# Conformer block on one core: transposed keys kept by pairs of tiles, and the scores of the last 32 keys computed in one run with the products of those keys

## Chip, core and metric

The kernel runs on one core of a Trainium2 chip. The metric is the device time of one launch in microseconds. Before the change three runs gave 1850.52, 1851.56 and 1852.84 us (median 1851.56). One further execution was taken with the hardware profiler; it took 1851.06 us, with a span of 1846.9 us between its first and its last profiled instruction.

## What is computed

Two sequences (B = 2) of T = 4000 tokens of width D = 512 go through one Conformer block, all in bf16:

```python
h = _silu(_layernorm(x) @ w_ff1_a) @ w_ff1_b;  x1 = x + 0.5 * h
h = _layernorm(x1);  q, k, v = h @ w_q, h @ w_k, h @ w_v
p = _softmax(einsum('btd,bsd->bts', q, k) * D ** -0.5)
x2 = x1 + einsum('bts,bsd->btd', p, v) @ w_o
# then a gated convolution of width 3 with normalization over all tokens (x3),
# a second feed-forward half step (x4), and a last _layernorm
```

The part that matters here is the attention: every token's query against all 4000 keys of its sequence. 4000 is 31 tiles of 128 keys and one tile of 32, so there are 32 key tiles and the last one has only 32 keys.

## The kernel before

**Stages.** The work goes in 16 chunks of 512 tokens (the eighth and the sixteenth have 416), eight per sequence. All chunks go through the first feed-forward half (until about 430 us of the span). Then comes attention, chunk by chunk, g = 0 to 15, mixed with the projections and convolutions of earlier chunks (about 440 to 1346 us), then the rest of the convolution and the second feed-forward half.

**Attention.** `attention` (line 2255) runs for each chunk g over 32 steps kt, one per key tile. Chunk 0 is done plainly, tile by tile (`scores`, line 1822). In the other chunks four key tiles make a "quad", and the scores of a quad are formed with seven products in place of eight (`score_quad`, line 2184, four steps; `half_quad`, line 2146, does it for tiles 0 and 1). The seven products use the transposed keys `hT` themselves and sums of them, `KF`, which VectorE forms once per sequence (`k_sums`, line 2101), which are stored in DRAM (`kfd`) and loaded again for each chunk (`k_stream`). Within `score_quad`, product 5 (`KF` by a sum of queries, both in the region `xt`) goes into bank 1 of PSUM (called `s` in the profile), ScalarE copies it away, and products 6 and 7 wait for additions of VectorE. Exponentials go into the region `sums`, and the products with the values (`pv`, line 1962) go into banks `y`, and one into the fourth bank of `s`.

**The tile of 32 keys.** Its scores are computed by `tail_scores` (line 2438): 16 matmuls in which the stationary operand is only 32 columns wide, four of them side by side in the array, each for a quarter of the queries (`tile_position=(0, j * REST)`; the profile calls this form 128*32). They go into bank 1; ScalarE takes the exponential into `pq` (region `wff`), which is stored in DRAM (`pqd`) and read back by four DMAs into `ptail`, laid out for the next use. That use is `pv_rest` (line 1982) with tail = 1: products with the values of those 32 keys, contracted over 32 rows, three of them side by side for u = 0 and three for u = 1 (`tile_position=(j * REST, 0)`; form 32*128). `pv_rest` for chunk g runs in `late_second` (line 2333), that is at step kt = 1 of chunk g + 1, and once more at kt = 6 for one product that uses all rows. `tail_scores` for chunk g runs at kt = 24 of chunk g (21 in chunk 0, 16 in the last).

**Transposed keys.** The normalized rows of all tokens are stored in DRAM (`keysd`). `key_queries` (line 2469) brings one tile of 128 keys into `hT` with one DMA transpose on SP's queue, [128 keys, 512] into [128, 4, 128]. `hT` of a chunk is laid out tile by tile. The first 20 tiles of sequence 0 come during the first feed-forward half, the rest in its last chunk and at the start of attention; the tiles of sequence 1 replace those of sequence 0 during g = 7 and 8 (`keys_swap`, line 2402).

**Order.** Nothing is issued in the order of the code. `Plan` (line 112) collects all operations with their dependences and estimated costs and lists them anew for each engine; operations on TensorE that belong to one accumulation (`inc` false up to the last) make one block and are not separated. Each engine then runs its list in order, so an instruction that waits holds back all behind it on its engine; this holds for the DMAs that SP issues, too. Nearly every instruction is recorded under line 95, so groups are told apart by the names of regions and by form.

The functions that the diff touches and their callers:

Of the kernel before, what the change touches and what calls it, by code (L numbers as in the profile page):

```python
# [15 lines left out]
TILE = 128  # L16
TPC = 4
# [3 lines left out]
FC = F // 128  # L21
# [538 lines left out]
class Conformer:  # L560
# [35 lines left out]
    def memory(self):  # L596
# [55 lines left out]
        self.b_hT = [[A.buf("hT%d" % t, t * 4096 + j * 1024, 1024) for j in range(TPC)]  # L652
                     for t in range(TCB)]
# [62 lines left out]
        self.hv = A.view(TCB * 4096, 2 * PAIRS * D).rearrange("p (n k e d) -> p n k e d", k=2, e=2, d=HD)  # L716
        self.hq = A.view(2048, QUADS * 2048).rearrange("p (q u r e j k) -> p q u r e j k", q=QUADS, u=2, r=2, e=2, j=2)
        self.hh = A.view(0, 1024).rearrange("p (r e n) -> p r e n", r=2, e=2)
        self.kfd = nc.dram_tensor("kfd", [B, QUADS + 1, 128, 1536], BF16, kind="Internal").ap()
# [1038 lines left out]
    def row_max(self, qc):  # L1758

        S, s = self.S, qc % 2  # L1760
        for ti in range(TPC):
            for kc in range(TCB):
                ps, b_ps = self.sbank()
                out = ps[0:TILE, :].rearrange("p (t k) -> p t k", t=TPC)
                for cc in range(DC):
                    self.mm(out, self.qT[s][:, cc, ti * TILE:(ti + 1) * TILE], self.hT[kc][:, :, cc, :],
                            cc == 0, cc == DC - 1, [self.b_qT[s][cc]] + self.b_hT[kc], b_ps)
# [54 lines left out]
    def scores(self, g, kt, bank=None):  # L1822
        s, W = g % TCB % 2, width(g)
        kc, kj = divmod(kt, TPC)
        ps, b_ps = bank or self.sbank()
        for cc in range(DC):
            self.mm(ps[:, 0:W], self.hT[kc][:, kj, cc, :], self.qT[s][:, cc, 0:W],
                    cc == 0, cc == DC - 1 and not self.any_score,
                    [self.b_hT[kc][kj], self.b_qT[s][cc]], b_ps)
# [270 lines left out]
    def k_sums(self, g, q, step):  # L2100
# [5 lines left out]
        if q < 0:  # L2106
            a11, a12, a21, a22 = [self.hh[:, r, e] for r in range(2) for e in range(2)]
            s1, s2, s4 = [self.KF[n][:, m, 0].rearrange("p j k -> p (j k)") for m in range(3)]
# [36 lines left out]
    def half_quad(self, g, step):  # L2145
# [5 lines left out]
        m5, b_m5 = self.m5h[:, 0:hw], self.b_m5h  # L2151
        part = lambda r, e: (lambda j: self.hT[0][:, r, 2 * e + j, :], self.b_hT[0][r])
        form = lambda m: (lambda j: self.KF[0][:, m, 0, j], self.b_KF[0][m])
# [88 lines left out]
    def attention(self, old, hook, between):  # L2242

        S = self.S
        for g in range(NCK):
            W, plain = width(g), g == 0
            for kt in range(KT):
# [157 lines left out]
    def keys_swap(self, g, kt):  # L2405
# [31 lines left out]

    def tail_scores(self, g):

# [3 lines left out]
        ps, b_ps = self.bank(1)  # L2443
        hT, b_hT = self.hT[TCB - 1][:, TPC - 1], self.b_hT[TCB - 1][TPC - 1]
        parts = [(slice(j * REST, (j + 1) * REST), slice(j * n, (j + 1) * n)) for j in range(4)]
# [4 lines left out]
        if self.any_score:  # L2450
            for j, (r, q) in enumerate(parts):
# [3 lines left out]
        self.store(self.pqd[:, 0:n], self.pq[:, 0:n], [self.b_pq], [self.b_pqd])  # L2455
        k = S.dsems[self.nxt("ld", 16)]
        src = self.pqd[:, 0:n].rearrange("(j k) q -> k j q", j=4)
        S.dma("SP", k, *[lambda e, r=r: e.dma_start(self.ptail[r, 0:W].rearrange("p (j q) -> p j q", j=4), src)
                         for r, q in parts], reads=[self.b_pqd], writes=[self.b_ptail])

# [8 lines left out]
    def key_queries(self, b, kt):  # L2469
        kc, kj = divmod(kt, TPC)  # L2470
        src, rd = self.key_source(b, kt)
        self.transpose(self.hT[kc][:, kj], src, rd, [self.b_hT[kc][kj]])

# [461 lines left out]
    def program(self, any_score):  # L2935
# [37 lines left out]
        def key_rest():  # L2973

            for k in range(self.PRELOAD, 28):
                yield 8, lambda k=k: self.key_queries(0, k)
            for k in range(15):
                yield 11, lambda k=k: self.key_values(0, k)
            for k in range(28, KT):
                yield FC, lambda k=k: self.key_queries(0, k)  # L2980
# [5 lines left out]
        def ff1(c):  # L2986
            def hook(f):
# [369 lines left out]
```

## Time and profile before

| | |
|---|---|
| three timed runs | 1850.52, 1851.56, 1852.84 us |
| profiled execution | 1851.06 us (span 1846.9 us) |
| TensorE (PE) busy | 1827.6 us, 16082 matmuls |
| VectorE (DVE) busy | 1491.3 us |
| ScalarE (ACT) busy | 1364.9 us |
| DMA | 231.09 MB, mean 125 GB/s |
| DMA transposes of 128 keys | 62 out of `keysd`, 2 out of `tailsd` |

Times are microseconds from the start of the span. In a timeline row stand the start, the duration, the engine, the line, the operation, out<-in by region names, the form and the count; in brackets follows idle time before the instruction with what ended it. A matmul is written as (rows*columns of the array), then the moving operand. Consecutive matmuls overlap, so the time that one costs is read from the distance between starts, not from its duration. For a group, the first number after the bar is its busy time, the second the mean duration in ns of one instruction.

### The profile page before, as it was taken

How to read it: one execution, taken by the hardware profiler on the slowest of the kernel's cores; microseconds unless marked ns; L12 is line 12 of the kernel's file. 1: busy time of each engine (PE TensorE's matmuls, PEld its weight loads, DVE VectorE, ACT ScalarE, POOL GpSimd, SP SyncE). 2: the span in 40 equal slices, each digit the busy share in tenths (PEclk: the TensorE clock that was granted, in tenths of full speed). 3: DMA queues.
4: the chain of work that ended last, by engine and by line, in shares of the span. 5: the costliest groups of instructions: out<-in, count | busy, mean ns of one | idle time of the engine just before them, and what ended most of it. 6: DMA issues, size and time to landing. Idle time of an engine off the chain costs nothing.

```text
span 1846.9 us, 40836 instructions
## 1 busy us (share of the span) xinstructions
PE 1827.6 (99%) x16082; PEld 1518.8 (82%) x16168; DVE 1491.3 (81%) x3240; ACT 1364.9 (74%) x2433; POOL 144.3 (8%) x357
## 2 busy tenths in 40 slices
PE   9999999999999999999999999999999999999998
PEld 6888888866888888889878888888876888888887
DVE  8889898868766877677876777777779989889886
ACT  6887777755656877787777877887768788777775
POOL 2000000000000000000100000000011000000010
PEclk9999999999999999999999999999999999999999
DMA  7332344287645655458954444543476222211211
GB/s 200 87 91 85 83 111 100 70 245 226 173 144 143 189 153 157 125 151 178 241 146 136 123 116 117 146 122 111 124 218 171 56 69 77 73 47 48 64 44 45
DMA packets 317722, 231.09 MB, mean 125 GB/s; under 512 B 191362, under 2 KB 288325, under 8 KB 317268
## 3 DMA queue, kind: packets, MB, share of 16 engines
q1 hardware_dynamic: 316996, 228.15, 45.7%
q8 instruction: 129, 2.11, 0.5%
q14 instruction: 69, 0.57, 0.1%
q10 hardware_dynamic: 528, 0.26, 0.0%
HBM read 131.15 MB, written 56.22 MB: 101 GB/s over the span
## 4 chain that ended last, share of the span: by engine, by line
PE 95%; DVE 2%; ACT 1%; DMA 1%; issue 1%; SPq 0%; DVEq 0%; ACTq 0%
PE y L95 50%; PE s L95 45%; DVE work L95 1%; ACT work L95 0%; DVE wff L95 0%; ACT sums L95 0%; DMA work<-work 0%; DMA pqd<-wff 0%; ACT keys L95 0%; DVE xt L95 0%; DVE sums L95 0%; DVE s L95 0%; DMA xt<-kfd 0%; DVE keys L95 0%; ACT xt L95 0%
## 5 line engine op out<-in xcount | busy, mean ns | idle before, releaser
L95 ACT ACTIVATE sums<-s 128x512 bf16<-128x512 f32 (+4 forms) x498 | 291.3, 586 | 145.9 <-PE s L95 143.0
L95 ACT ACTIVATE keys<-s 128x512 bf16<-128x512 f32 (+3 forms) x275 | 156.9, 574 | 132.7 <-PE s L95 101.6
L95 DVE TENSOR_TENSOR sums<-sums 128x512 bf16<-128x512 bf16 (+3 forms) x528 | 201.3, 399 | 54.6 <-ACT sums L95 42.2
L95 PE MATMUL y<-work,keys 128*128 128x256 bf16 x1920 | 244.4, 273 | 0.0
L95 PE MATMUL s<-sums 128*128 128x256 bf16 (+1 forms) x1428 | 212.6, 272 | 0.1
L95 PE MATMUL y<-sums,keys 128*128 128x256 bf16 (+1 forms) x1440 | 210.6, 270 | 0.0
L95 PE MATMUL y<-wff,keys 128*128 128x256 bf16 (+2 forms) x1590 | 209.4, 276 | 0.1
L95 ACT ACTIVATE work<-xt,work 128x512 bf16<-128x512 bf16 x260 | 199.5, 784 | 9.5 <-DVE work L95 7.8
L95 PEld LDWEIGHTS y<-work,keys 128*128 128x128 bf16 x1920 | 187.8, 98 | 22.4
L95 PE MATMUL y<-work,wff 128*128 128x256 bf16 (+3 forms) x1324 | 197.2, 272 | 0.1
L95 DVE TENSOR_TENSOR keys<-keys 128x1024 bf16<-128x1024 bf16 (+2 forms) x264 | 170.7, 660 | 22.9 <-ACT keys L95 20.2
L95 PE MATMUL s<-work,keys 128*128 128x256 bf16 (+4 forms) x1329 | 184.6, 275 | 1.0
L95 PEld LDWEIGHTS y<-wff,keys 128*128 128x128 bf16 (+1 forms) x1592 | 151.4, 98 | 30.2 <-issue 3.4
L95 DVE BATCH_NORM_STATS2 work<-xt 128x6 f32<-128x512 bf16 x251 | 164.3, 681 | 2.4 <-DMA xt<-in_x_dram 1.7
L95 PEld LDWEIGHTS s<-sums 128*128 128x128 bf16 x1428 | 139.0, 98 | 22.5 <-DVE s L95 0.4
L95 PEld LDWEIGHTS y<-sums,keys 128*128 128x128 bf16 x1440 | 138.1, 98 | 21.3 <-issue 2.9
L95 POOL TENSOR_TENSOR work<-work 128x4 f32<-128x4 f32 (+3 forms) x108 | 91.2, 845 | 764.8 <-DVE work L95 741.8
L95 PE MATMUL s<-xt,keys 128*128 128x256 bf16 (+1 forms) x924 | 142.3, 270 | 1.2 <-DVE s L95 1.1
L95 PEld LDWEIGHTS y<-work,wff 128*128 128x128 bf16 x1324 | 127.3, 98 | 17.6 <-DVE wff L95 0.4
L95 PE MATMUL y<-sums,xt 128*128 128x256 bf16 (+1 forms) x960 | 140.7, 270 | 0.3 <-DVE sums L95 0.3
L95 PEld LDWEIGHTS s<-work,keys 128*128 128x128 bf16 (+1 forms) x1348 | 107.7, 97 | 34.9 <-ACT sums L95 2.2
L95 PE MATMUL s<-xt 128*128 128x256 bf16 (+1 forms) x893 | 131.4, 270 | 1.3 <-DMA xt<-kfd 0.9
(163 smaller groups left out, 3343.9 us busy)
## 6 DMA issues: line engine op xcount, KB each, us to landing
xt<-kfd SPq DMA_DIRECT2D x98, 384.0 KB, 3.2
xt<-v12d SPq DMA_DIRECT2D x105, 256.0 KB, 3.1
xd<-xt SPq DMA_DIRECT2D x28, 512.0 KB, 2.7
xt<-xd SPq DMA_DIRECT2D x28, 512.0 KB, 3.8
out_dram<-xt SPq DMA_DIRECT2D x14, 512.0 KB, 2.9
xt<-in_x_dram SPq DMA_DIRECT2D x13, 512.0 KB, 4.4
dcvd<-wff SPq DMA_DIRECT2D x48, 128.0 KB, 2.9
keys<-dcvd SPq DMA_DIRECT2D x12, 512.0 KB, 3.7
```

The source lines that it names most:

```text
L95: return getattr(eng, self.name)(*self.args, **self.kw)
```

## The change

Two things change, and the rest of the diff adapts addresses to them.

1. `hT` is laid out by pairs of tiles, [2 pairs, 4, 2 tiles, 128], and a new `key_pair` brings 256 keys with one DMA transpose, [256, 512] into [128, 4, 256]. The two last tiles of a sequence are still brought singly. The times at which the plan's input lists these loads shift by a few steps, and the 32-key tile of sequence 1 is listed for step 5 of chunk 7 where it was step 6 of chunk 8. The sums of keys now read runs of 128 elements where they read 256.
2. `tail_scores` of chunk o + 1 is called in `late_second(o)`, right behind `pv_rest` of chunk o, and `pv_rest` no longer ends its accumulations with `inc`, so that both make one block for the plan. The four DMAs that read `pqd` back are listed eight steps later. Chunk 0 keeps its call at kt = 21.

```diff
-        self.hT = [A.view(t * 4096, 2048).rearrange("p (t c k) -> p t c k", t=TPC, c=DC)
-                   for t in range(TCB)]
+        self.hTp = [A.view(t * 4096, 2048).rearrange("p (m c x) -> p m c x", m=2, c=DC) for t in range(TCB)]
+        self.hT = [A.view(t * 4096, 2048).rearrange("p (m c r k) -> p m r c k", m=2, c=DC, r=2) for t in range(TCB)]
...
-    def pv_rest(self, g, tail, ns):
+    def pv_rest(self, g, tail, ns, inc=None):
...
-                        False, u == 1, [b, b_x], b_ps, skip_group_check=True, **at)
+                        False, u == 1, [b, b_x], b_ps, inc=inc, skip_group_check=True, **at)
...
-            a11, a12, a21, a22 = [x[:, :, r, e].rearrange("p u j k -> p u (j k)") for r in range(2) for e in range(2)]
-            s1, s2, s4 = [self.KF[n][:, m].rearrange("p u j k -> p u (j k)") for m in range(3)]
+            a11, a12, a21, a22 = [x[:, :, r, e] for r in range(2) for e in range(2)]
+            s1, s2, s4 = [self.KF[n][:, m] for m in range(3)]
...
-                if kt == (21 if g == 0 else 24 if g < NCK - 1 else 16):
+                if g == 0 and kt == 21:
                     self.tail_scores(g)
...
         self.pv(o, 7, self.group(GROUPS - 1))
-        for tail in range(2):
-            self.pv_rest(o, tail, (7, 3, 2))
+        self.pv_rest(o, 0, (7, 3, 2))
+        if o < NCK - 1:
+            self.pv_rest(o, 1, (7, 3, 2), False)
+            self.tail_scores(o + 1, 8)
+        else:
+            self.pv_rest(o, 1, (7, 3, 2))
...
-            for k in range(KT):
-                if (6 + k * (2 * KT - 20) // KT if k < KT - 1 else KT + 6) == at:
-                    self.key_queries(1, k)
+            for k in range(0, KT - 2, 2):
+                if 7 + k * (2 * KT - 20) // KT == at:
+                    self.key_pair(1, k)
+            for k in range(2):
+                if at == (7 + (KT - 2) * (2 * KT - 20) // KT, 5)[k]:
+                    self.key_queries(1, KT - 2 + k)
...
-    def tail_scores(self, g):
+    def tail_scores(self, g, back=0):
...
+        def load():
+            k = S.dsems[self.nxt("ld", 16)]
+            S.dma("SP", k, *[lambda e, r=r: e.dma_start(self.ptail[r, 0:W].rearrange("p (j q) -> p j q", j=4), src)
+                             for r, q in parts], reads=[self.b_pqd], writes=[self.b_ptail])
+
+        if back:
+            self.after(back, load)
+        else:
+            load()
...
+    def key_pair(self, b, kt):
+        kc, kj = divmod(kt, TPC)
+        src, rd = self.keys_at(b, kt * 128, 256)
+        self.transpose(self.hTp[kc][:, kj // 2], src, rd, self.b_hT[kc][kj:kj + 2])
...
-            for k in range(self.PRELOAD, 28):
-                yield 8, lambda k=k: self.key_queries(0, k)
+            for k in range(self.PRELOAD, 28, 2):
+                yield 8, lambda k=k: self.key_pair(0, k)
...
-                if TCB < c < NCK - 1 and f % 4 == 2:
-                    k = (c - TCB - 1) * 4 + f // 4
+                if TCB < c < NCK - 1 and f % 8 == 2:
+                    k = (c - TCB - 1) * 4 + f // 8 * 2
                     if k < self.PRELOAD:
-                        self.key_queries(0, k)
+                        self.key_pair(0, k)
```

What this does to the lists of the engines is shown at two places. The first is TensorE's list at kt = 1 of chunk 4 (641 to 643 us of the profile before). `y<-xt,keys` and `s<-xt,keys` are the tile before the last (`pv_rest` with tail = 0), `y<-wff,keys` and `s<-wff,keys` the 32-key products, `s<-work,keys 32x128` the scores of the 32 keys; `s<-xt 128x256` with three more is product 5 of the first quad (into bank 1), the pair `s<-xt` and the two `s<-work,keys` are products 6 and 2 of `half_quad`, and `s<-xt,keys` behind the wait for VectorE is its product 7. Before:

```order
L95 MATMUL s<-xt 128x256 [waits cnt_ACT,dma_7]
L95 MATMUL s<-xt 128x256 x3
L95 MATMUL s<-xt,keys 128x256
L95 MATMUL y<-xt,keys 128x256
L95 MATMUL s<-xt 128x256 [waits cnt_ACT]
L95 MATMUL s<-xt 128x256
L95 MATMUL s<-work,keys 128x256 x2
L95 MATMUL y<-wff,keys 128x256 [waits dma_4]
L95 MATMUL s<-wff,keys 128x256
L95 MATMUL y<-wff,keys 128x256 x2
```

After those come the two last 32-key products, `y<-sums,keys 128x256 x6` and product 7. Now the same stretch reads:

```order
L95 MATMUL y<-wff,keys 128x256 [waits dma_9]
L95 MATMUL s<-wff,keys 128x256
L95 MATMUL y<-wff,keys 128x256 x2
L95 MATMUL s<-wff,keys 128x256
L95 MATMUL y<-wff,keys 128x256
L95 MATMUL s<-work,keys 32x128 [waits cnt_ACT]
L95 MATMUL s<-work,keys 32x128 x15
L95 MATMUL y<-sums,keys 128x256 x2
L95 MATMUL s<-xt 128x256 [waits cnt_ACT]
L95 MATMUL s<-xt 128x256
L95 MATMUL s<-work,keys 128x256 x2
L95 MATMUL s<-xt 128x256 [waits cnt_ACT,dma_7]
```

The 16 score matmuls stand directly behind the six 32-key products; products 6 and 2 and product 5 have moved behind both, and four `y<-sums,keys` follow before product 7. At kt = 24 the 16 matmuls are gone; in the feed-forward halves TensorE's list is the same as before.

The second place is SP's list of DMAs around kt = 24 to 31 of chunk 14 (about 1298 to 1309 us). `pqd<-wff` stores the exponentials of the 32 keys, `wff<-pqd` reads them back, `xt<-kfd` loads the sums of a quad of keys, `xt<-v12d` sums of values. Before:

```order
L95 DMA xt<-xd 128x2048 [waits dma_36]
L95 DMA pqd<-wff 128x128 [waits cnt_ACT]
L95 DMA xt<-v12d 128x2x512 [waits cnt_PE,dma_0]
L95 DMA wff<-pqd 32x4x128 [waits dma_37]
L95 DMA wff<-pqd 32x4x128 x3
L95 DMA xt<-kfd 128x1536 [waits cnt_PE,dma_1]
```

And now the same stretch with what follows it, up to the load of the last chunk's 32-key exponentials:

```order
L95 DMA xt<-xd 128x2048 [waits dma_37]
L95 DMA xt<-v12d 128x2x512 [waits cnt_PE,dma_1]
L95 DMA xt<-kfd 128x1536 [waits cnt_PE]
L95 DMA dcvd<-wff 128x512 [waits cnt_DVE]
L95 DMA xt<-v12d 128x512 [waits cnt_PE,dma_4]
L95 DMA xt<-v12d 128x2x512 [waits cnt_PE,dma_6,dma_11]
L95 DMA pqd<-wff 128x104 [waits cnt_ACT]
L95 DMA xt<-kfd 128x1536 [waits cnt_PE]
L95 DMA dcvd<-wff 128x512 [waits cnt_DVE]
L95 DMA lrowd<-wff 1x512 [waits cnt_DVE]
L95 DMA work<-lrowd 128x4 [waits dma_39]
L95 DMA xt<-kfd 128x1536 [waits cnt_PE]
```

The four reads of `pqd`, with their wait for the store, no longer stand ahead of the load of `kfd`; they come behind this piece, with other work between the store and them.

More of the change, by code (lines that the diff above doesn't have):

```diff
@@ L649, in memory @@
         self.b_h = [A.buf("h%d" % k, o + k * 1024, 1024) for k in range(KT)]
-        self.hT = [A.view(t * 4096, 2048).rearrange("p (t c k) -> p t c k", t=TPC, c=DC)
-                   for t in range(TCB)]
-        self.b_hT = [[A.buf("hT%d" % t, t * 4096 + j * 1024, 1024) for j in range(TPC)]
+        self.hTp = [A.view(t * 4096, 2048).rearrange("p (m c x) -> p m c x", m=2, c=DC) for t in range(TCB)]
+        self.hT = [A.view(t * 4096, 2048).rearrange("p (m c r k) -> p m r c k", m=2, c=DC, r=2) for t in range(TCB)]
+        self.b_hT = [[A.bufs("hT%d" % t, [(t * 4096 + j // 2 * 2048 + cc * 512 + j % 2 * 256, 256) for cc in range(DC)])
+                      for j in range(TPC)]
                      for t in range(TCB)]
@@ L1763, in row_max @@
                 ps, b_ps = self.sbank()
-                out = ps[0:TILE, :].rearrange("p (t k) -> p t k", t=TPC)
+                out = ps[0:TILE, :].rearrange("p (m r k) -> p m r k", m=2, r=2)
                 for cc in range(DC):
-                    self.mm(out, self.qT[s][:, cc, ti * TILE:(ti + 1) * TILE], self.hT[kc][:, :, cc, :],
+                    self.mm(out, self.qT[s][:, cc, ti * TILE:(ti + 1) * TILE], self.hT[kc][:, :, :, cc, :],
                             cc == 0, cc == DC - 1, [self.b_qT[s][cc]] + self.b_hT[kc], b_ps)
@@ L2107, in k_sums @@
             a11, a12, a21, a22 = [self.hh[:, r, e] for r in range(2) for e in range(2)]
-            s1, s2, s4 = [self.KF[n][:, m, 0].rearrange("p j k -> p (j k)") for m in range(3)]
+            s1, s2, s4 = [self.KF[n][:, m, 0] for m in range(3)]
             b_x = self.b_hT[0][0:2]
@@ L2455, in tail_scores @@
         self.store(self.pqd[:, 0:n], self.pq[:, 0:n], [self.b_pq], [self.b_pqd])
-        k = S.dsems[self.nxt("ld", 16)]
         src = self.pqd[:, 0:n].rearrange("(j k) q -> k j q", j=4)
-        S.dma("SP", k, *[lambda e, r=r: e.dma_start(self.ptail[r, 0:W].rearrange("p (j q) -> p j q", j=4), src)
-                         for r, q in parts], reads=[self.b_pqd], writes=[self.b_ptail])
+        def load():
[6 more added lines that the diff above has]
+            load()
     def key_source(self, b, kt):
@@ L2973, in key_rest @@
         def key_rest():
-            for k in range(self.PRELOAD, 28):
-                yield 8, lambda k=k: self.key_queries(0, k)
+            for k in range(self.PRELOAD, 28, 2):
+                yield 8, lambda k=k: self.key_pair(0, k)
             for k in range(15):
                 yield 11, lambda k=k: self.key_values(0, k)
-            for k in range(28, KT):
+            yield FC, lambda: self.key_pair(0, 28)
+            for k in range(30, KT):
                 yield FC, lambda k=k: self.key_queries(0, k)
```

12 lines of the change are left out of this document (6 added, 6 removed).

## The prediction

> **What bounds the kernel now.** I read the page first: the busy times, the slices and the chain that ended last.
>
> ```profile
> span 1846.9 us, 40836 instructions
> PE 1827.6 (99%) x16082; PEld 1518.8 (82%) x16168; DVE 1491.3 (81%) x3240; ACT 1364.9 (74%) x2433; POOL 144.3 (8%) x357
> PEclk9999999999999999999999999999999999999999
> PE 95%; DVE 2%; ACT 1%; DMA 1%; issue 1%; SPq 0%; DVEq 0%; ACTq 0%
> ```
>
> TensorE is the bound from end to end, at full granted clock. Idle it can lose at most 1846.9 - 1827.6 = 19.3 us in the whole span. The change lists TensorE's work differently in attention alone, so I read that stretch by windows, and two stretches of the first feed-forward half, where key transposes run beside it.
>
> ```profile
> 440.00:1346.00 906.00, 900.39 (x8198) 756.04 (x8242) 683.23 (x1559) 668.72 (x1247) 55.98 (x212) 1.00 0.56 149
> 200.00:300.00 100.00, 100.00 (x919) 89.64 (x917) 90.32 (x185) 78.62 (x132) 8.05 (x8) 1.00 0.43 102
> 300.00:400.00 100.00, 99.95 (x870) 84.95 (x869) 82.44 (x172) 66.78 (x114) 7.91 (x14) 1.00 0.46 126
> ```
>
> After the length stand the busy times of PE, PEld, DVE, ACT and POOL. TensorE idles 906.0 - 900.4 = 5.6 us in attention and nothing in the feed-forward stretch. A gain must therefore come out of matmul time that looks busy, or out of those 5.6 us.
>
> **The price of a narrow run.** Busy hides something here: the ends of matmuls are modelled, so I take distances between starts. Two timelines of PE, first a plain run of 12, then one chunk's 16 score matmuls of the 32 keys:
>
> ```profile
> 836.01 1.47 PE L95 MATMUL y<-sums,work 128*128 128x256 bf16 x12
> 837.32 0.38 PE L95 MATMUL s<-work,wff 128*128 128x256 bf16 x2
> ...
> 627.05 0.60 PE L95 MATMUL s<-xt,keys 128*128 128x256 bf16 x4
> 627.58 0.41 PE L95 MATMUL s<-work,keys 128*32 128x128 bf16 x16
> 627.92 0.39 PE L95 MATMUL y<-sums,xt 128*128 128x256 bf16 x2
> ```
>
> Twelve full matmuls of 256 columns take 837.32 - 836.01 = 1.31 us, 0.109 us each. Four from 627.05 should end at 627.49; the narrow run starts at 627.58, 0.09 us late. It then takes 0.34 us to the next full matmul, where four rounds of 128 columns, at half of 0.109 us, are 0.22: another 0.12 us. The 32-row products show the same, here in the next chunk:
>
> ```profile
> 641.47 0.38 PE L95 MATMUL s<-work,keys 128*128 128x256 bf16 x2
> 641.78 0.28 PE L95 MATMUL y<-wff,keys 32*128 32x256 bf16 x1
> ...
> 641.91 0.27 PE L95 MATMUL y<-wff,keys 32*128 32x256 bf16 x1
> 642.11 0.83 PE L95 MATMUL y<-sums,keys 128*128 128x256 bf16 x6
> 642.85 0.39 PE L95 MATMUL s<-xt,keys 128*128 128x256 bf16 x2
> ```
>
> Two full ones from 641.47 should end at 641.69; the run starts at 641.78, and the next full matmul at 642.11, where two rounds of 0.109 us would have ended at 642.00. So 0.09 in, 0.11 out. I take **0.10 us for each change of form**, 0.20 us for a run.
>
> **Term 1, the runs that join.** The 16 score runs are one per chunk:
>
> ```profile
> L95 PE MATMUL s<-work,keys 128*32 128x128 bf16 x224 | 5.7, 222 | 0.0
> L95 PE MATMUL s<-work,keys 128*32 128x104 bf16 x32 | 0.7, 212 | 0.0
> ```
>
> 256 matmuls in sixteens. The 32-key products are also one run per chunk, except that twice the plan had put full matmuls into the middle, which is paid as one more run. Both places, the first with its neighbours:
>
> ```profile
> 825.79 0.38 PE L95 MATMUL y<-wff,keys 32*128 32x256 bf16 x2
> 826.10 0.35 PE L95 MATMUL s<-xt 128*128 128x208 bf16 x2
> 826.29 0.34 PE L95 MATMUL s<-work,keys 128*128 128x208 bf16 x2
> 826.56 0.28 PE L95 MATMUL s<-wff,keys 32*128 32x256 bf16 x1
> ...
> 1310.60 0.53 PE L95 MATMUL s<-work,keys 128*128 128x208 bf16 x4
> 1311.06 0.28 PE L95 MATMUL y<-wff,keys 32*128 32x256 bf16 x1
> ```
>
> Before: 16 + 16 + 2 = 34 runs, 68 changes of form. Now: 15 joined runs, the lone scores of chunk 0 and the lone products of chunk 15, that is 17 runs with 34 outer changes; the block keeps them whole, so the two splits go. The unknown is the step inside a joined run, from 32 rows to 32 columns. The trace has no such step. Its ends: 0 (the array is already divided) gives 34 fewer changes, -3.4 us; the price of leaving one form and entering the other through the full one, 0.20 us, gives 68 - 34 - 30 = 4 fewer, -0.4 us. The nearest row is any change of form, 0.10 us, so I take that: 68 - 49 = 19 fewer, **-1.9 us**.
>
> The Trainium skill, "TensorEngine Tiling (Array Packing)", section "Key Properties", says that changing the tiling mode, and not just the tile, drains the TensorE. By that rule 32 rows to 32 columns is a change of mode like any other, and the sum is -1.9 us rather than -3.4; the 0.09 to 0.12 us at the four edges above agree with it, while no run here shows the inner step.
>
> **Term 2, a wait behind the 32-key round trip.** The waits of SP's queue and two timelines, SP and PE, at the end of chunk 14:
>
> ```profile
> SPq L95 <- DMA pqd<-wff: 16.9, 11, 4.2
> ...
> 1299.09 0.42 SPq L95 DMA_DIRECT2D pqd<-wff  x1
> ...
> 1304.17 1.75 SPq L95 DMA_DIRECT2D wff<-pqd  x4
> 1306.02 0.42 SPq L95 DMA_DIRECT2D xt<-kfd  x1
> ...
> 1308.14 0.34 PE L95 MATMUL s<-work,xt 128*128 128x208 bf16 x2
> 1309.42 0.53 PE L95 MATMUL s<-xt 128*128 128x208 bf16 x4 [0.94 <-DMA xt<-kfd]
> ```
>
> SP stores the exponentials, then stands until 1304.17 for the store to land, issues four reads in 1.75 us, and only then the load of key sums, for which TensorE idles 0.94 us. It is the one DMA wait of TensorE in attention; elsewhere the same queueing (11 waits, 16.9 us) is hidden by loads that are early enough. In the changed list that load stands ahead of the reads, and eight steps lie between store and reads, so the wait goes: **-0.9 us**, the ends 0 and -0.94. What is late next there is VectorE and ScalarE, which both waited for TensorE after the gap, so nothing steps in. The four reads, 1.75 us of SP, now pass kt = 9; a quad's sums are loaded some 8 us before use (four steps of 62 us / 32) and land in about 3 us, which covers them.
>
> **Term 3, what is queued behind the joined run.** Its first score matmul waits until ScalarE has emptied bank 1. That copy precedes product 5, which stood in this place before without a wait, so nothing. Product 5 must now wait for the exponential of the 32 keys. The rows:
>
> ```profile
> L95 ACT ACTIVATE wff<-s 128x128 bf16<-128x128 f32 x14 | 3.8, 274 | 1.6 <-PE s L95 1.6
> ...
> 643.07 0.38 PE L95 MATMUL s<-work,xt 128*128 128x256 bf16 x2
> ...
> 643.49 0.60 ACT L95 ACTIVATE sums<-s 128x512 bf16<-128x512 f32 x1 [1.67 <-PE s L95]
> ```
>
> From the start of the 16: they end 0.41 us later, ScalarE needs 0.27 us, and two handovers some 0.05 each (643.07 + 0.38 for the matmuls to 643.49 for the copy is 0.04): bank 1 is free at 0.78. TensorE goes on at 0.34 with two `y`, products 6 and 2 (six matmuls, 0.65 us) and comes to product 5 at 0.99, 0.21 us to spare. ScalarE idles 1.67 us there, so the exponential starts at once. In chunk 1 only four matmuls cover (0.78 against 0.78). I take **0**; the upper end is a 0.60 us copy ahead of the exponential in every chunk, 15 x (0.78 + 0.60 - 0.99) = +5.9 us. Product 7, behind VectorE's addition (it began 0.07 us late at 642.85), keeps enough in front of it; the addition's own wait may gain or lose 0.1 us a chunk, taken as 0.
>
> **Terms at nothing.** Fewer, longer transposes and other patterns for VectorE. The rows give SP's issue (least, median, most, in ns), the landing times in us, and two groups of VectorE:
>
> ```profile
> L95 SPq DMA_TRANSPOSE keys<-keysd x62: 1188/1267/2305, 207.3 to 912.0; - x62
> L95 SPq DMA_TRANSPOSE work<-keysd x16: 1308/2685/4618, 375.5 to 1197.6; - x16
> ...
> keys<-keysd SPq DMA_TRANSPOSE x62, 3.6
> work<-keysd SPq DMA_TRANSPOSE x16, 4.9
> ...
> L95 DVE TENSOR_TENSOR xt<-keys 128x512 bf16<-128x512 bf16 x21 | 8.8, 417 | 0.5 <-issue 0.3
> L95 DVE TENSOR_TENSOR s<-s,xt 128x512 f32<-128x512 f32 x103 | 71.9, 698 | 53.3 <-PE s L95 47.8 <-ACT xt L95 3.9 <-PE y L95 0.2
> ```
>
> 128 rows take SP 1.27 us, 512 rows 2.69; a pair I estimate at 1.7 (a third of the way), so SP saves 30 x 0.84 = 25 us of a queue that TensorE does not wait for. What hides it is that tiles come far ahead of use; the uncovered price is a rival below. VectorE's key sums now read runs of 128; the exact pattern is not in the trace, the bounds are one key sum of 512 at its present 0.42 us and the same at the 0.70 us of the f32 group, 4 x 14 quads x 0.28 = 16 us on an engine that idles 223 us in attention. I take no change.
>
> **Sum.** -1.9 - 0.9 = -2.8 us, -0.15%. The profiled execution took 1851.06 us (span 1846.9 and 4.2 around it), 0.5 us below the median 1851.56 of the three. 1851.06 - 2.8 = 1848.3, from the median 1848.8; I forecast **1848.5 us**, with 1847.0 to 1850.5 as its own range (terms 1 and 2 at their small ends; 0.7 us for waits that fall otherwise).
>
> **Rivals.**
> - *The step inside is free, or more waits fall away.* Then term 1 is -3.4, and with product 7's waits gone about -4.5 in all: 1847. For it: both runs use the divided array. Against it: each edge in the trace costs the same whichever form is entered. 20%.
> - *The saved time becomes waiting.* VectorE and ScalarE are three quarters busy in attention, and a wait of 0.1 to 0.2 us in each chunk for bank 1 or for VectorE, 15 x 0.19, takes back the 2.8 us: 1851.5. The change would then not do what it says. For it: the small slack in chunk 1 and the 0.07 us at 642.85; against it: ScalarE's 1.67 us idle. 18%.
> - *Slower: pairs hold up the transposes of the layer norms* in the first feed-forward half. Those (`work<-work`) share SP's queue, and a pair lands up to 4.9 - 3.6 = 1.3 us later than a single tile. With ten pairs in chunks 9 to 14 that is up to +13 us on VectorE's sums and then TensorE: at half of it 6.5 - 2.8 = +3.7, 1855; in full 1861. It decides when the slack of those transposes is under 0.6 us. Against it: TensorE idles 0.05 us in 200 us there although single tiles already stand in that queue. 9%; the full bank-1 wait of term 3 (1854.6) has another 3%.
>
> **How the numbers follow.** Forecast 50%, rivals 20, 18, 9 and 3. A measurement of this kernel can tell about 0.2%, 3.7 us, from no change: below 1847.9 or above 1855.3. Faster by more: the free step's 20% and 6% of the forecast's low edge, 26%. Slower by more: the 9% of the transposes and 3%, 12%. The rest, 62%, is within. The range takes in the free step and the waiting rival and leaves out the slow tail: 1845.5 to 1853.5.
>
> **What would show it.** In the profile after: the 16 scores directly behind the 32-row products, with about 0.2 us from the start of the last three of those to the first score (0.10 if the inner step is free); product 5 without idle time; no wait for `kfd` near 1309; SP's waits for `pqd` near zero; TensorE still without idle time from 200 to 400 us. The forecast is wrong if `s<-xt` waits for ScalarE behind every joined run, or if TensorE waits in the feed-forward half.

## The result, and the profile after

The kernel after takes 1848.32 us (median of 22 runs, 1846.19 to 1850.77), the kernel before, over as many runs, 1851.95 us (1850.20 to 1854.12). The ratio is 0.9979, with a 95% interval of 0.9973 to 0.9986: 2.6 to 5.0 us faster, and by the medians 3.6. The forecast was 1848.5 us, from a sum of -2.8 us. The profiled execution took 1848.09 us.

The page of the kernel after begins as before, with a span that is 2.9 us shorter (1846.9 before) and TensorE at 99%:

```profile
span 1844.0 us, 40792 instructions
PE 1824.8 (99%) x16082; PEld 1519.9 (82%) x16168; DVE 1493.0 (81%) x3240; ACT 1367.4 (74%) x2433; POOL 146.0 (8%) x357
```

The windows of the kernel after, the same stretches as in the prediction (length, then busy PE, PEld, DVE, ACT, POOL):

```profile
440.00:1346.00 906.00, 901.20 (x8236) 760.78 (x8280) 686.42 (x1564) 674.81 (x1253) 57.23 (x212) 1.00 0.55 150
200.00:300.00 100.00, 100.00 (x918) 89.63 (x917) 90.43 (x185) 78.67 (x131) 8.05 (x8) 1.00 0.45 102
300.00:400.00 100.00, 99.95 (x871) 85.03 (x871) 82.62 (x172) 67.13 (x115) 7.70 (x16) 1.00 0.51 131
```

The feed-forward stretches are as full as they were, so the slower rival did not happen: longer transposes do not hold up TensorE there. Attention's idle time went from 5.6 to 4.8 us; the rest of the gain has to lie in time that looks busy. There it is, at a joined run in TensorE's timeline of the kernel after, chunk 4:

```profile
640.16 0.27 PE L95 MATMUL y<-xt,keys 128*128 128x256 bf16 x1
640.36 0.28 PE L95 MATMUL y<-wff,keys 32*128 32x256 bf16 x1
...
640.49 0.27 PE L95 MATMUL s<-wff,keys 32*128 32x256 bf16 x1
640.49 0.27 PE L95 MATMUL y<-wff,keys 32*128 32x256 bf16 x1
640.69 0.41 PE L95 MATMUL s<-work,keys 128*32 128x128 bf16 x16
641.02 0.39 PE L95 MATMUL y<-sums,keys 128*128 128x256 bf16 x2
...
641.47 0.38 PE L95 MATMUL s<-work,keys 128*128 128x256 bf16 x2
641.69 0.60 PE L95 MATMUL s<-xt 128*128 128x256 bf16 x4
```

From the last three products (640.49) to the first score (640.69) are 0.20 us, 0.11 of them a round of 256 columns: the inner step costs about 0.09 us, as the way in (640.16 to 640.36, less 0.11) does. Product 5, the four `s<-xt` at 641.69, starts 0.22 us after the two matmuls ahead of it, without idle time.

To add this up I took, for each narrow run, the distance from the start of the full matmul ahead of it to the start of the full one behind it, less what the matmuls take at their pace. One score run costs 0.211 us over its matmuls, one product run 0.204, a joined run 0.319; a product run that the plan split cost 0.508. Over attention that is 7.89 us before and 5.84 us after (both with another run of narrow matmuls at 910 us, 0.84 to 0.85 us in every kernel, that the change leaves alone): **-2.05 us**. The other piece is the wait at the end of chunk 14. SP's timeline of the kernel after, and TensorE's:

```profile
1297.70 0.37 SPq L95 DMA_DIRECT2D xt<-v12d  x1
1300.28 0.32 SPq L95 DMA_DIRECT2D xt<-kfd  x1
...
1307.37 0.32 SPq L95 DMA_DIRECT2D pqd<-wff  x1
```

```profile
1307.33 0.60 PE L95 MATMUL y<-sums,keys 128*128 128x256 bf16 x4
1307.77 0.52 PE L95 MATMUL s<-xt 128*128 128x208 bf16 x4
```

The load of key sums goes out at 1300.28 instead of 1306.02, and the `s<-xt` that needs it (1307.77) no longer waits: start to start **-1.10 us**, of which 0.94 were idle. Waits of SP for `pqd` are gone from its list (16.9 us before). The two add up to -3.15 us against a span that is 2.9 us shorter: all other gains and losses of these two executions come to about +0.2 us. That sum looked closed. It was not.

### The profile page after: what moved, and what is told of

The parts are those of the page before. It is cut to its first block, busy times and chain, and to the rows that moved or that the text cites. A ratio compares the mean times of both kernels' runs of the same rounds, so it can differ in the third digit from the quotient of the medians.

```text
span 1844.0 us, 40792 instructions
## 1 busy us (share of the span) xinstructions
PE 1824.8 (99%) x16082; PEld 1519.9 (82%) x16168; DVE 1493.0 (81%) x3240; ACT 1367.4 (74%) x2433; POOL 146.0 (8%) x357
## 4 chain that ended last, share of the span: by engine, by line
PE 92%; DVE 4%; ACT 2%; DMA 1%; issue 1%; POOL 0%; SPq 0%; DVEq 0%; ACTq 0%
PE y L95 48%; PE s L95 44%; DVE work L95 1%; ACT work L95 1%; DVE sums L95 1%; DMA work<-work 1%; DVE keys L95 1%; ACT keys L95 0%; DVE xt L95 0%; ACT sums L95 0%; DVE wff L95 0%; DMA dcvd<-wff 0%; DMA xt<-v12d 0%; DVE s L95 0%; DMA xt<-in_x_dram 0%
```

## The experiments

**First theory:** the gain is the changes of form (-2.05 us) and the load of key sums (-1.1 us); pairs of tiles are worth nothing; what remains is the chance of the order, since the plan puts instructions elsewhere after any edit. **Rival:** the relief of SP's queue by pairs carries part of the gain. Each run was timed against the kernel before on its own chip (median of before 1851.5 us in the first eight, 1852.1 in the next three, 1852.4 in the last), 11 runs each; the interval of a ratio is about +-0.0009, 1.7 us. The last column is what narrow runs cost in attention, added up as above.

| run | us, median | ratio to before, 95% | narrow runs, us |
|---|---|---|---|
| pairs alone | 1849.96 | 0.9993 (0.9984-1.0002) | 7.89 |
| joined run alone | 1850.36 | 0.9994 (0.9985-1.0003) | 5.84 |
| reads later, alone | 1851.98 | 1.0000 (0.9991-1.0009) | 7.89 |
| after, scores apart | 1850.16 | 0.9990 (0.9981-0.9999) | 7.50 |
| after, reads at once | 1848.67 | 0.9980 (0.9971-0.9989) | 5.84 |
| after, more changes of form | 1851.39 | 0.9997 (0.9988-1.0006) | 9.17 |
| before, reads by GpSimd | 1850.12 | 0.9990 (0.9981-0.9999) | 7.90 |
| before, other order | 1853.77 | 1.0009 (1.0000-1.0018) | 7.89 |
| after, other order | 1848.41 | 0.9980 (0.9971-0.9989) | 5.84 |
| pairs alone, other order | 1850.07 | 0.9988 (0.9979-0.9997) | 7.89 |
| joined alone, other order | 1851.23 | 0.9996 (0.9987-1.0005) | 5.84 |
| after, single tiles in chunks 7, 8 | 1850.61 | 0.9992 (0.9983-1.0001) | 5.84 |

### More changes of form

Only the order inside the joined run differs from the kernel after:

```diff
-            self.pv_rest(o, 1, (7, 3, 2), False)
-            self.tail_scores(o + 1, 8)
+            self.tail_scores(o + 1, 8, o)
...
         for cc in range(DC):
+            if o is not None and cc % 2 == 0:
+                self.pv_rest(o, 1, (7, 3, 2), False, (cc // 2,))
```

> The kernel after, with the same 22 narrow matmuls of each joined run in the order three products, eight scores, three products, eight scores: 30 more changes of form, none through the full form, and nothing else. Theory (every change of form costs about 0.10 us, whichever forms): each joined run costs 0.51 to 0.53 us over its matmuls instead of 0.32, +3.0 us in all, 1851.3 us. Rival (only the way into and out of the divided array costs; what the trace of after shows inside the run is the last matmuls' own time): 1848.3 us, as the kernel after.

TensorE's timeline of this kernel at the same run:

```profile
641.05 0.27 PE L95 MATMUL y<-xt,keys 128*128 128x256 bf16 x1
641.25 0.28 PE L95 MATMUL y<-wff,keys 32*128 32x256 bf16 x1
...
641.47 0.29 PE L95 MATMUL s<-work,keys 128*32 128x128 bf16 x8
641.70 0.28 PE L95 MATMUL y<-wff,keys 32*128 32x256 bf16 x1
...
641.91 0.29 PE L95 MATMUL s<-work,keys 128*32 128x128 bf16 x8
642.14 0.39 PE L95 MATMUL y<-sums,keys 128*128 128x256 bf16 x2
```

641.25, 641.47, 641.70, 641.91, 642.14: every half takes 0.21 to 0.23 us where its matmuls take 0.11. The narrow runs cost 9.17 us instead of 5.84, 3.32 us for 30 changes, 0.111 us each, and the time is 3.1 us above the kernel after (+3.0 expected). So a change of form costs about the same inside a joined run as at its edges.

### Scores apart

```diff
+            if kt == 2 and o < NCK - 1:
+                self.tail_scores(o + 1, 7)
```

with `late_second` as before.

> The kernel after, with the 16 scores taken out of the run with the products and listed one step later (kt = 2) as a run of their own; the reads stay delayed. Each of 15 chunks then has four changes of form instead of three. Theory: 15 x 0.10 = +1.5 us against the kernel after, up to +1.9 if the plan splits runs again: 1849.8 to 1850.2 us. Rival A (the inner step from 32 rows to 32 columns is what costs, leaving by the full form is nearly free): 1848.3 us, as the kernel after. Rival B (the place at kt = 1 also mattered, for the waits of products 5 and 7): 1851 us or more.

1850.16 us; the narrow runs cost 7.50 us, 1.65 more than after, for 16 more changes (one product run was split, one pair stayed joined by the plan's choice). The time is what the theory gave, and the trace refutes rival A. The load of key sums in chunk 14 was not waited for here either.

### Reads later, alone

In the kernel before, `self.tail_scores(g, 4)` at the old place, with the reads listed four steps later.

> The kernel before, with the four reads of the 32-key exponentials listed four steps later and nothing else. Theory: SP's 11 waits for the store (16.9 us) go, TensorE's wait for the load of key sums at 1309 us goes, -0.9 us: 1851.0 us. Rival A (the order as a whole, not this wait, made the gain): 0.0 +- 0.4, 1851.5 to 1852.3 us. Rival B (the queueing cost TensorE more than the one wait in the profile shows, and the term was sized too small): -1.5 us or more, 1850.4 us or less.

This changed almost nothing: 1851.98 us where 1851.0 was expected. SP's timeline:

```profile
1298.69 0.42 SPq L95 DMA_DIRECT2D pqd<-wff  x1
1299.21 0.38 SPq L95 DMA_DIRECT2D xt<-v12d  x1
1303.73 1.75 SPq L95 DMA_DIRECT2D wff<-pqd  x4
1305.59 0.38 SPq L95 DMA_DIRECT2D xt<-kfd  x1
```

The plan takes transfers up to 16 us ahead of where they are listed, so SP's order here stayed what it was, with 17.0 us of waiting for the store and TensorE's wait at 1309 us. The run says nothing of the wait's price, but it says that listing the reads four steps later does not by itself remove the wait.

### Reads at once, in the kernel after

`self.tail_scores(o + 1)` in place of `self.tail_scores(o + 1, 8)`.

> The kernel after, with the four reads of the 32-key exponentials listed directly behind the store instead of eight steps later. Theory (the standing queue costs TensorE only where a load behind it is due): SP's waits for the store come back, some 10 us and more in all; TensorE loses 0 to 1 us, in one or two stalls on a load of sums, 1848.3 to 1849.3 us. Rival (the standing queue costs in every chunk): 15 x 0.2 = +3 us, 1851.3 us.

SP waits for the store 3 times, 4.0 us in all, where 10 us and more were expected, and the time is 1848.67 us, as after. Between the new place (kt = 1) and the first use of the reads lie some 60 us instead of 17 (nine steps of kt), and the plan, which goes by what is needed first, puts other transfers ahead of them by itself.

### Reads by GpSimd, in the kernel before

```diff
-        S.dma("SP", k, *[lambda e, r=r: e.dma_start(self.ptail[r, 0:W]...
+        S.dma("POOL", k, *[lambda e, r=r: e.dma_start(self.ptail[r, 0:W]...
```

with a semaphore of its own for `k`.

> The kernel before, with the four reads issued by GpSimd's queue instead of SP's; runs, layout and transposes stay as before. Theory: SP no longer waits for the store (16.9 us, 11 times), the load of key sums in chunk 14 goes out about 5 us earlier, TensorE's wait at 1309 us goes: 0.9 to 1.1 us less of waiting there, and other waits within 0.5 us of before: 1850.6 us against 1851.5. Rival A (the load is late for another reason): the wait at 1309 us stays, 1851.5 us. Rival B: the re-planned order around it gives waits of the same size elsewhere, 1851 to 1852.5 us though that one wait is gone.

SP's timeline of this kernel, and TensorE's where it waited before:

```profile
1298.49 0.43 SPq L95 DMA_DIRECT2D pqd<-wff  x1
1299.02 0.39 SPq L95 DMA_DIRECT2D xt<-v12d  x1
1301.66 0.32 SPq L95 DMA_DIRECT2D xt<-kfd  x1
```

```profile
1306.49 0.60 PE L95 MATMUL y<-sums,keys 128*128 128x256 bf16 x4
1306.93 0.52 PE L95 MATMUL s<-xt 128*128 128x208 bf16 x4
```

The load goes out 4.4 us earlier than before and nothing waits for it. The time is 1850.12 us, 0.2 to 3.5 under the kernel before by the ratio (1850.6 was expected). The standing queue was the cause of that wait.

### Pairs alone, and joined run alone

The first is the kernel after with the scores' run as before; the second the kernel before with the joined run (and the tile with the 32 keys of the second sequence listed at step 5, as after, since its scores now come earlier).

> The kernel after, with the 32-key scores back in their own place at kt = 24 and their reads directly behind the store; only the layout by pairs and the transposes of 256 rows are left of the change. Theory (the gain is fewer changes of form and the reads that no longer hold up SP): nothing, 1851.5 to 1852.5 us, 0.0 +- 0.5 against the kernel before, though SP's queue issues some 20 to 25 us less of transposes. Rival A (the relief of SP's queue carries part of the gain): 1850.5 us or less. Rival B (the sums of keys in runs of 128 cost VectorE, and the other part hides it): 1853 us or more, with the group of key sums above 0.50 us each.

> The kernel before with the joined run and the reads eight steps later; layout and transposes stay by single tiles. Theory: the whole of the change, -2.8 to -3.6 us, 1848.3 to 1849.1 us. Rival A (pairs carry part): -2 us or less of a gain, 1850 us or more. Rival B: under 1847.8 us, the pairs had cost something.

Both went against the theory. Pairs alone gave 1849.96 us, 1.5 under the kernel before, though TensorE's wait for the key sums was still there (1.2 us start to start) and the narrow runs cost the same. VectorE's sums of keys, which now read runs of 128, took 418 ns each as against 417, so the prediction's term for them is nothing, as it took it. The joined run alone gave 1850.36 us, a gain of 1.1 us where 2.8 to 3.6 were expected, though the narrow runs cost what they do in the kernel after and the wait for the key sums is gone. Either the order's chance is this large, or pairs matter.

### Another order

One number of the planner, in four kernels (before, after, pairs alone, joined alone):

```diff
-    SPARE = 3000
+    SPARE = 2800
```

> The kernel before, with one number of the planner changed, the spare time of a transfer from 3000 to 2800: the same instructions, in an order that differs in places. It measures what the order alone is worth. Theory (the part of the gain beyond changes of form and the one wait is the chance of the order): the sum of TensorE's waits between 440 and 1345 us moves by 0.5 to 1.5 us either way, the price of narrow runs stays at 7.9 us, 1850.0 to 1853.0 us. Rival (the waits belong to the kernel's structure and stay): the same waits at the same places within 0.3 us in all, 1851.5 us.

> The kernel after, with the planner's spare time of a transfer at 2800 instead of 3000. Theory (changes of form are worth 2.05 us in any order, the wait for key sums about 1 us, the rest is the chance of the order): 2 to 5 us under the kernel before at 2800 (1853.8), so 1849 to 1852 us; the price of narrow runs 5.84 us as in after. Rival (the gain depends on this one order): within 1 us of the kernel before at 2800, 1853 us or more.

> Pairs of tiles alone (the run of scores and its reads as in the kernel before), with the planner's spare time at 2800. Theory (pairs are worth nothing; 1850.0 at 3000 was the chance of the order): the sum of TensorE's waits is no smaller than in the kernel before at 3000 on average, 1851 to 1854 us. Rival (pairs relieve SP's queue and so shorten waits): again about 1.5 to 2 us under the kernel before at the same 2800, 1852.2 us or less.

> The joined run alone (single tiles), with the planner's spare time at 2800. Theory: about 3 us under the kernel before at 2800 (1853.8), give or take 1.5 for the order: 1849.3 to 1852.3 us; price of narrow runs 5.84 us. Rival (joining without pairs is worth 1 us only, as 1850.4 against 1851.5 at 3000 had it): 1852.8 us or more.

| median us | runs apart, 3000 | apart, 2800 | joined, 3000 | joined, 2800 |
|---|---|---|---|---|
| single tiles | 1851.95 | 1853.77 | 1850.36 | 1851.23 |
| pairs | 1849.96 | 1850.07 | 1848.32 | 1848.41 |

The order alone moved the kernel before by about 2 us and the others by under 1. Two expectations missed by little: the kernel before in the other order came out 0.8 us above its range, the kernel after 0.6 us below. Pairs are faster by 2.0, 3.7, 2.0 and 2.8 us (mean 2.6), joined runs by 1.6, 2.5, 1.6 and 1.7 (mean 1.9). These medians are of several chips; with each kernel taken against the kernel before on its own chip, pairs are faster by 1.5, 4.2, 2.5 and 2.8 us (mean 2.8) and joined runs by 1.1, 3.1, 2.1 and 1.7 (mean 2.0). One such difference is known to about 2 us, a mean of four to about 1 (an estimate from those intervals). The intervals hold the scatter of executions and not the chance of the order, which each pair of kernels has anew; that all four differences have one sign speaks against chance. **That pairs are worth nothing is refuted.** And joining is worth about 2 us, less than the 3.15 us that its two pieces come to in the profiles.

Where? For each kernel I summed what TensorE loses between the starts of successive full matmuls (pieces over 0.06 us; edges of narrow runs and missing records left out):

| us lost by TensorE | 840 to 950 us | 950 to 1300 us | 1300 to 1312 us |
|---|---|---|---|
| single tiles, apart (before, other order, reads later, reads by GpSimd) | 1.9 to 2.7 | 1.0 | 1.1; 0 with reads by GpSimd |
| pairs, apart (two orders) | 1.4, 1.6 | 0.4, 0.3 | 1.2, 1.1 |
| single tiles, joined (two orders) | 4.3, 4.2 | 0.8, 0.9 | 0 |
| pairs, scores at kt = 1 or 2 (after, four variants) | 1.4 to 2.1 | 0.1 to 0.8 | 0 to 0.1 |

The stretch from 840 to 950 us lies in chunks 7 and 8, where the transposes of the second sequence's keys are listed. With joined runs it holds some 2.2 us, most of what pairs are worth there. With the runs apart it holds only 0.5 us (order 3000) and 1.1 us (order 2800); another 0.6 us lies in the second column, and 0.8 to 1.1 us in one wait of TensorE for VectorE near 1611 us, which pairs alone do not have. So the table places the gain of pairs in these chunks for joined runs alone.

There VectorE shows what is late. SP's timeline of the kernel before, and VectorE's; `lrowd` carries the row sums to memory and back (128x4):

```profile
886.75 0.33 SPq L95 DMA_DIRECT2D lrowd<-wff  x1
887.13 3.82 SPq L95 DMA_TRANSPOSE keys<-keysd  x3
890.99 0.58 SPq L95 DMA_DIRECT2D keys<-vhd  x1
891.62 2.51 SPq L95 DMA_TRANSPOSE keys<-keysd  x2
894.17 0.58 SPq L95 DMA_DIRECT2D work<-lrowd  x1
```

```profile
881.56 0.42 DVE L95 TENSOR_TENSOR work<-work 128x512 bf16<-128x512 bf16 x1 [1.15 <-DMA work<-work]
...
898.67 0.18 DVE L95 RECIPROCAL work<-work 128x4 f32<-128x4 f32 x1 [0.54 <-DMA work<-lrowd]
```

Between the store of the row sums and their load stand five key transposes, 6.3 us of SP's queue, and VectorE waits 0.54 us for the load; ahead of that it waits 1.15 us for a transpose of a layer norm. Between the two, TensorE waits for VectorE:

```profile
885.67 0.22 PE L95 MATMUL s<-xt 128*128 128x96 bf16 x1 [0.21 <-DVE wff L95]
```

The same place with pairs alone, SP's timeline:

```profile
884.98 0.26 SPq L95 DMA_DIRECT2D lrowd<-wff  x1
885.28 1.24 SPq L95 DMA_TRANSPOSE keys<-keysd  x1
886.56 0.59 SPq L95 DMA_DIRECT2D keys<-vhd  x1
887.20 4.04 SPq L95 DMA_TRANSPOSE work<-keysd  x1
891.28 0.58 SPq L95 DMA_DIRECT2D work<-lrowd  x1
```

The load goes out at 891.28 and nobody waits for it. VectorE's wait for this load, near 899 us, stands in the trace of five of the seven kernels that transpose these keys by single tiles (0.54 to 1.61 us; the last of them is below) and in one of the seven with pairs, the kernel after with reads at once (0.13 us).

### Single tiles in chunks 7 and 8 only

A **second theory** follows: single tiles crowd SP's queue in chunks 7 and 8, and what stands behind them there makes VectorE late, and TensorE with it. The kernel after, with the second sequence's keys by single tiles, listed a step earlier than the pairs, as in the kernel before:

```diff
-            for k in range(0, KT - 2, 2):
-                if 7 + k * (2 * KT - 20) // KT == at:
-                    self.key_pair(1, k)
-            for k in range(2):
-                if at == (7 + (KT - 2) * (2 * KT - 20) // KT, 5)[k]:
-                    self.key_queries(1, KT - 2 + k)
+            for k in range(KT):
+                if (6 + k * (2 * KT - 20) // KT if k < KT - 1 else 5) == at:
+                    self.key_queries(1, k)
```

> The kernel after, except that the keys of the second sequence (listed in chunks 7 and 8) are transposed by single tiles again; layout, pairs of the first sequence, joined runs and delayed reads stay. First theory (transposes by pairs cost and save nothing; what differs is the chance of the order): 1848.3 +- 1 us, TensorE's waits from 840 to 950 us near the 2.0 of after. Second theory, formed from the runs so far (single tiles crowd SP's queue in chunks 7 and 8, so that transposes of layer norms and the load of the row sums go out late, VectorE waits for them and TensorE for VectorE): VectorE waits about 1.4 us for the row sums near 899, TensorE's waits from 840 to 950 us rise to about 4.2 us as in the joined run alone, +2.2 us: 1850.5 us.

The time is 1850.61 us, as the second theory had it, and 4.3 us are lost from 840 to 950 us (4.2 expected, 2.0 in after). VectorE's timeline of this kernel, and TensorE's:

```profile
853.37 0.43 DVE L95 TENSOR_TENSOR wff<-work 128x512 bf16<-128x512 bf16 x1 [1.27 <-DMA dcvd<-wff]
...
881.41 1.80 DVE L95 TENSOR_TENSOR work<-work 128x512 bf16<-128x512 bf16 x4 [1.34 <-DMA work<-work]
...
899.27 0.18 DVE L95 RECIPROCAL work<-work 128x4 f32<-128x4 f32 x1 [0.68 <-DMA work<-lrowd]
```

```profile
854.52 0.53 PE L95 MATMUL s<-work,keys 128*128 128x208 bf16 x4 [1.01 <-DVE xt L95]
887.02 0.22 PE L95 MATMUL s<-xt 128*128 128x96 bf16 x1 [0.52 <-DVE wff L95]
900.69 0.61 PE L95 MATMUL y<-work,wff 128*128 128x256 bf16 x4 [0.28 <-DVE wff L95]
```

Read in pairs: behind each wait of VectorE for a transfer comes one of TensorE for VectorE, 1 to 6 us later. The chain that ended last runs through all three; here is its first passage, from a store of the convolution to TensorE:

```profile
849.71 3.56 DMA dcvd<-wff
...
853.37 0.43 DVE wff L95
853.79 0.68 DVE xt L95 x2
...
854.52 0.53 PE s L95 x4
```

The row sums make TensorE wait least of the three; the store of the convolution (`dcvd`) makes it wait most. VectorE's wait for the row sums was 0.68 us, not the 1.4 expected.

What of this comes from SP's queue? I compared the traces of all fourteen kernels.

- The store of the convolution goes out 25.5 to 25.9 us after the 32-row products at the start of chunk 7 (near 825 us) in the three kernels with single tiles and joined runs, this one among them, and after 24.2 to 24.9 us in the other eleven. So it is some 1.2 us late here. But order has a part in it: in every kernel with pairs VectorE's list has the operation that waits for this store a few instructions later.
- The store of the row sums goes out 1.6 to 2.2 us after VectorE has made them in the same three kernels, 0.1 to 1.1 us in the other four with single tiles, and at once (0.03 us) in all seven with pairs.
- The transposes of layer norms are not late here: the last one that VectorE waits for goes out at 877.20 us, as against 877.28 in the kernel after. This part of the second theory fails.

So two of the three transfers are late in SP's queue; how much of TensorE's loss belongs to them and how much to VectorE's other order is not separated. From 950 to 1300 us this kernel loses only 0.1 us, so the table's second column is not put down to the transposes of the second sequence. By time alone this run and the kernel after are just not told apart (0.9983 to 1.0001 against 0.9973 to 0.9986); the trace tells them apart by the stretch from 840 to 950 us.

## Why the prediction came out right, and where it was wrong

- **The bound.** Right: TensorE, and the two feed-forward stretches did not move.
- **Term 1, -1.9 us.** Right in its mechanism, -2.05 us measured. The inner step, which the trace of before did not have, costs 0.10 to 0.11 us like any other change. The 0.15 us beyond the forecast come from the two split runs: each split run cost 0.30 us more than a whole one, not 0.20. The Trainium skill, "TensorEngine Tiling (Array Packing)", section "Key Properties", says that a change of the tiling mode drains the engine; here 32 rows to 32 columns cost 0.10 us and the repeated steps of the more-changes run 0.111 us each, so rule and trace agree.
- **Term 2, -0.9 us.** The wait and its cause were right: -1.1 us start to start, and it also goes when GpSimd issues the reads. The step that named what removes it was wrong: "eight steps lie between store and reads, so the wait goes". Four steps at the old place left SP's order as it was, and no delay at the new place did not bring the wait back. What fits both runs is how long after the store the reads are needed, since the plan's code sorts by that.
- **Term 3, 0.** Right: product 5 does not wait behind the joined run.
- **Terms at nothing.** This step failed: "SP saves 30 x 0.84 = 25 us of a queue that TensorE does not wait for". First in size: a pair costs SP no more than a single tile. SP's issue in the kernel after (least, median, most, in ns):

```profile
L95 SPq DMA_TRANSPOSE keys<-keysd x32: 1226/1260/2992, 207.7 to 902.9; - x32
```

  and the landing, in us:

```profile
keys<-keysd SPq DMA_TRANSPOSE x32, 4.8
```

  Before it was 62 times 1267 ns, landing after 3.6 us. So SP is relieved of 30 x 1.27 = 38 us. Second, and worse, in kind: TensorE itself waits for that queue only once in attention (term 2), but VectorE waits for it often, for transposes of layer norms, row sums and the convolution's store, and TensorE waits for VectorE. From 440 to 840 and from 950 to 1300 us SP is issuing 28 to 40% of the time, so there the queue has time. From 840 to 905 us, where half the key transposes stand together, it is issuing 89 to 94% of the time with single tiles and 72 to 78% with pairs. Pairs are worth 2.6 us by the four comparisons, about as much as the forecast's whole sum. With joined runs the loss stands in this stretch; with the runs apart most of it stands elsewhere, and there the cause is open.
- **Why the sum still held.** A second omitted term has the other sign: with single tiles, joining costs 2.0 us more from 840 to 950 us (4.2 against 1.9 to 2.7). The prediction saw that "the four reads, 1.75 us of SP, now pass kt = 9" and called them covered; that they collide there with the key transposes fits the timelines and the two late stores above, but the reads were not moved alone, so it is argued, not shown. Pairs take that loss back, so the kernels before and after lose nearly the same in that stretch (1.9 and 2.0 us), and the two terms that were counted look like the whole. So the number was right in part by luck: joining alone, for which the whole -2.8 us was forecast, gave about -2, and pairs, put at nothing, made up for it.
- **The rivals.** The free inner step is refuted. That the saved time becomes waiting happened in the joined run alone, by VectorE's waits in chunks 7 and 8, not by the small slacks of bank 1 that the prediction named. That pairs hold up the layer norms had the wrong sign: TensorE loses nothing more in the feed-forward stretches, and over the whole kernel pairs are faster, though a pair lands 1.2 us later than a single tile.
- **What stays open.** By the medians the gain is 3.6 us and the counted terms give 3.15; the difference is inside the interval. From 1420 us on, where no edit is, TensorE loses 0.8 to 1.9 us in every kernel but the two with pairs alone, which lose nothing; most of it is the wait near 1611 us, and no run here says why. The order's chance is of the size of the terms themselves, about 2 us in the one kernel where it showed most.

No version that was run beats the kernel after: reads at once and the other order give the same time within the interval.

## What to carry to other kernels

A queue that is rarely waited for by the engine at the bound can still be on its path at second hand, so read its load stage by stage and look for who waits for what stands behind. An edit to a planned kernel moves other waits too: the parts measured alone, and in a second order, showed a term that the before and after profiles, which added up, had hidden. And a busy engine's price of switching forms is read from distances between starts; joining two runs of different narrow forms saves one change of form in four, since the step between them costs like any other.

## What the runs showed of the hardware

A DMA transpose of 256 rows x 512 took SP's queue 1.26 us (median), as one of 128 rows did (1.27), while one into `work` of 512 rows took 2.67. The one of 256 rows landed after 4.8 us (median), the one of 128 rows after 3.6. A change of TensorE's array form cost 0.10 to 0.11 us, at the edges of a narrow run and between two narrow forms alike, and it is counted as busy.

In five of the fourteen profiled executions (scores apart, reads by GpSimd, pairs alone and joined alone in the other order, single tiles in chunks 7 and 8) TensorE's granted clock dropped for a few us near 1402 us. In the last of them it was 0.57 from 1401 to 1405 us, where it was 1.00 in the kernel after, and about twelve matmuls of 256 columns started 0.21 us apart instead of 0.11. Such an execution loses some 1.3 us there. The profiles of before and after are not among the five, and the stretches of the table lie elsewhere.
